# Attention and two MLP layers on one core: from interleaved attention to attention first

## The chip, the cores and the metric

One of the eight cores of a Trainium2 chip runs the whole program. The metric is device time in microseconds (us) of one execution, from the first to the last instruction plus what little lies around them. Five engines work side by side, each through its own queue in order: TensorE (PE; its weight loads are listed as PEld), VectorE (DVE), ScalarE (ACT), GpSimd (POOL) and SyncE (SP), which issues most of the DMAs. They meet at semaphores.

## The reference, cut to what matters

```
scores = scale * q @ k.T                      # 4 batches, 8 heads, 576 x 576, head size 64
scores = where(block_i >= block_j, scores, -1e9)   # blocks of 64 positions
attn   = exp(scores - max); attn = attn / (sum(attn) + 1e-9)
x      = (attn @ v) as (2304 tokens, 512)
# layer 1
h = x @ w_in;  g = h if h >= 1, 0 if h <= -1, else (h + 1)**2 / 4;  x = g @ w_out
# layer 2
h = x @ w_in2; g = h * cos(h);                                       out = g @ w_out2
```

Both layers go from 512 to 2048 and back. The four weight matrices arrive as 64-bit floats.

## The kernel before, in words

**Precision.** A 32-bit number is kept as a sum of two rounded parts, hi and lo, and a product of two numbers as hi·hi + hi·lo + lo·hi. So each MLP product is three matmuls.

**Attention.** Two heads are worked at a time: 4 batches x 4 head pairs give 16 pairs. `load` brings k, q and v of a pair; `prep` transposes k and q on TensorE and splits them: `Q[h]` holds q's hi in the head's 64 rows and its lo in the other 64, `K[h]` holds k's hi in both halves, `L[h]` holds k's lo and zeros. A pair has five units, query tiles of 128, 128, 128, 128 and 64 rows (the last holds both heads). `scores` multiplies `Q[h]` with `K[h]` (hi·hi and lo·hi in one) and with `L[h]` (hi·lo), and then adds the mask by a third, small bf16 product of `mk_l` and `mk_r` on the 64 columns that are masked. Then DVE takes the negated maximum, ACT the exponential with its sum (L373, L418), DVE the reciprocal. `p_trans` transposes the probabilities on TensorE, ACT copies them out of PSUM (L467), `pv` multiplies with v (L488). Where `late` holds, the division comes after that: a matmul with the identity spreads the reciprocals (L496) and DVE multiplies (L508); otherwise POOL scales the probabilities first (L386, L433). The result, split in hi and lo, is stored to DRAM as `x1d` (L518), one DMA per pair.

**The MLP.** Tokens are worked in blocks of 512 (and one of 256, tokens 2048 to 2303); a block has NF = 16 steps, one per 128 columns of the hidden layer. `mm1` (L596) makes one hidden tile from 12 matmuls, `act` applies the activation through ACT, DVE and POOL and splits the result into `gh` (POOL, L152) and `gl` (DVE, L155), and two steps later `mm2` (L660 in layer 1, L667 in layer 2) adds 12 matmuls into the accumulators.

**Weights.** Each of the 64 weight tiles (32 per layer) is converted from 64-bit floats by `w_convert`: ACT takes the upper words (L176) and the lower ones (L182; early ones on POOL, L178), DVE joins them in two steps (L191, L195), hi is rounded on POOL or ACT, POOL subtracts to get lo (L155). w_in of layer 1 stays in SBUF; the other three matrices go back to DRAM, and w_out is fetched again for each step through a ring of six slots (`fetch`), layer 2's w_in once.

**Order.** Each stage registers its later parts with `at(d, ...)`, due d ticks later; a tick is one piece of attention or MLP. The first 133 pieces of attention (`START`: five pairs and eight pieces) run alone with eight PSUM banks; then `zipped` runs 48 steps of layer 1 with the rest of attention between them, 1.2 and later 1.06 pieces per MLP piece, with three banks for attention and one for `h`. Then come the rest of layer 1 and layer 2. The table `jobs` says in which MLP steps a weight tile is converted: two per step in the first 14, later fewer, and none in steps 64 to 79, which are the 256-token block. From all that a scheduler makes one queue per engine, and an engine never leaves its queue's order.

## Time and profile before

| what | value |
|---|---|
| median of three runs | 1113.91 us (1112.87 to 1118.11) |
| the profiled execution | 1114.9 us, its span 1112.7 us |
| mean granted TensorE clock | 0.975 of full speed |
| busy | PE 1046.3 us, DVE 618.3, ACT 558.6, POOL 410.8 |
| moved by DMA | 200.63 MB |

How to read it: busy times are sums over the whole span, over stages that have different limits. A matmul counts as busy while it is anywhere in the pipeline, so two that overlap count their union, and a PE that is shown busy may still issue fewer columns than it could. The stages are told apart by the tables of windows further down.

### The profile page before, as it was taken

The numbers are of one execution on the slowest core, as the hardware profiler recorded it, in microseconds if no ns is written. First come the engines' busy times: TensorE is split into PE (matmuls) and PEld (weight loads), VectorE is DVE, ScalarE is ACT, GpSimd is POOL, SyncE is SP. The second block draws the span as 40 slices with busy tenths as digits, with TensorE's granted clock in tenths as the row PEclk, the third lists the DMA queues.
The fourth block names the chain that finished last, engine by engine and source line by source line (L and its number), as shares of the span: only waits on it lengthen the run. The fifth ranks groups of instructions, "written<-read, shape, count | busy, mean of one in ns | idle before, by whom it ended". The sixth has DMA issues, their size and how long they took to land.

```text
span 1112.7 us, 17002 instructions
## 1 busy us (share of the span) xinstructions
PE 1046.3 (94%) x5912; PEld 847.5 (76%) x5912; DVE 618.3 (56%) x1143; ACT 558.6 (50%) x1253; POOL 410.8 (37%) x577
## 2 busy tenths in 40 slices
PE   8888889999999979999949999899999999999998
PEld 6666667777777756777737889788888888888897
DVE  6677597676535455466507443254454454454464
ACT  6777688766445465555515433333333343343343
POOL 1234376554423444355507531132223222322322
PEclk8998999999999989999979999999999999999999
DMA  5576466557644584556786679722532442442353
GB/s 134 154 202 196 136 211 199 189 176 242 230 133 154 174 257 152 173 179 217 242 320 220 215 264 380 264 95 95 172 131 97 168 150 96 151 134 95 114 191 113
DMA packets 145572, 200.63 MB, mean 180 GB/s; under 512 B 66384, under 2 KB 107344, under 8 KB 145488
## 3 DMA queue, kind: packets, MB, share of 16 engines
q1 hardware_dynamic: 138576, 174.39, 48.8%
q0 software_dynamic: 6912, 25.17, 5.8%
q8 instruction: 47, 0.77, 0.3%
q14 instruction: 37, 0.30, 0.1%
HBM read 150.77 MB, written 48.76 MB: 179 GB/s over the span
## 4 chain that ended last, share of the span: by engine, by line
PE 72%; ACT 8%; DMA 8%; DVE 6%; issue 3%; SPq 2%; POOL 1%; POOLq 0%; ACTq 0%; DVEq 0%
PE h L596 32%; PE a L667 17%; PE a L660 12%; PE s L488 4%; DMA raw<-in_moe_w_in_dram 3%; PE s L350 3%; PE s L451 2%; DMA x1d<-xs 2%; ACT raw L182 2%; ACT raw L176 2%; ACT P L373 1%; PE s L299 1%; DVE wv L195 1%; DMA w2i<-w 1%; DVE raw L191 1%
## 5 line engine op out<-in xcount | busy, mean ns | idle before, releaser
L596 PE MATMUL h<-x,w 128*128 128x512 f32 (+1 forms) x1920 | 439.4, 377 | 28.1 <-DMA x<-x1d 13.9
L596 PEld LDWEIGHTS h<-x,w 128*128 128x128 f32 x1920 | 340.3, 192 | 95.1 <-DMA x2d<-y 14.3
L152 POOL TENSOR_SCALAR gh<-ea 128x512 fp32r<-128x512 f32 (+1 forms) x160 | 101.2, 632 | 394.1 <-DVE ea L640 177.4
L660 PE MATMUL a<-gh,w 128*128 128x512 f32 (+1 forms) x640 | 199.7, 376 | 0.0
L667 PE MATMUL a<-w,gh 128*128 128x512 f32 x576 | 174.3, 390 | 0.1
L155 DVE TENSOR_TENSOR gl<-ea,gh 128x512 fp32r<-128x512 f32 (+1 forms) x160 | 123.2, 770 | 82.5 <-POOL gh L152 81.9
L660 PEld LDWEIGHTS a<-gh,w 128*128 128x128 f32 x640 | 116.0, 189 | 18.3 <-issue 0.7
L636 ACT ACTIVATE eb<-eb 128x512 f32<-128x512 f32 (+1 forms) x80 | 47.0, 588 | 158.7 <-DVE eb L633 158.7
L667 PEld LDWEIGHTS a<-w,gh 128*128 128x128 f32 x576 | 107.1, 188 | 22.0 <-POOL gh L152 0.5
L615 ACT ACTIVATE ea<-h,half 128x512 f32<-128x512 f32 (+1 forms) x80 | 51.6, 644 | 141.4 <-PE h L596 134.6
L660 PE MATMUL a<-gl,w 128*128 128x512 f32 (+1 forms) x320 | 120.8, 377 | 0.0
L667 PE MATMUL a<-w,gl 128*128 128x512 f32 x288 | 108.4, 389 | 0.0
L640 DVE TENSOR_TENSOR ea<-h,eb 128x512 f32<-128x512 f32 (+1 forms) x80 | 50.8, 637 | 79.7 <-ACT eb L637 79.7
L629 POOL TENSOR_SCALAR ea<-ea 128x512 f32<-128x512 f32 (+1 forms) x80 | 64.1, 801 | 79.0 <-ACT ea L626 76.3
L155 POOL TENSOR_TENSOR w<-wv,w 128x512 fp32r<-128x512 f32 x64 | 87.5, 1369 | 13.1 <-ACT w L210 11.2
L191 DVE SCALAR_TENSOR_TENSOR raw<-raw 128x512 uint32<-128x512 uint32 x64 | 49.4, 772 | 74.5 <-ACT raw L182 72.2
L626 ACT ACTIVATE ea<-h,magic 128x512 f32<-128x512 f32 (+1 forms) x80 | 51.3, 642 | 78.2 <-PE h L596 64.3
L488 PE MATMUL s<-PT,rv 128*64 128x128 f32 (+2 forms) x960 | 73.8, 274 | 16.5 <-ACT P L418 6.1
L632 DVE TENSOR_TENSOR eb<-h,ea 128x512 f32<-128x512 f32 (+1 forms) x80 | 51.0, 637 | 57.3 <-POOL ea L629 57.3
L373 ACT ACTIVATE P<-s,m 128x512 f32<-128x512 f32 (+3 forms) x128 | 66.5, 524 | 31.2 <-DVE m L366 30.0
L621 DVE SCALAR_TENSOR_TENSOR ea<-ea,h 128x512 f32<-128x512 f32 (+1 forms) x80 | 50.4, 630 | 54.9 <-ACT ea L618 54.0
L488 PEld LDWEIGHTS s<-PT,rv 128*64 128x64 f32 (+1 forms) x960 | 50.5, 140 | 39.1 <-issue 10.6
(87 smaller groups left out, 1425.9 us busy)
## 6 DMA issues: line engine op xcount, KB each, us to landing
w<-w2o SPq DMA_DIRECT2D x80, 512.0 KB, 3.3
w<-w1o SPq DMA_DIRECT2D x64, 512.0 KB, 4.5
raw<-in_moe_w_in_dram SPq DMA_DIRECT2D x32, 512.0 KB, 4.7
raw<-in_moe_w_out_dram SPq DMA_DIRECT2D x32, 512.0 KB, 5.1
x1d<-xs SPq DMA_DIRECT2D x16, 576.0 KB, 4.5
x2d<-y SPq DMA_DIRECT2D x36, 256.0 KB, 6.4
x<-x2d SPq DMA_DIRECT2D x36, 256.0 KB, 5.5
w1o<-w POOLq DMA_DIRECT2D x16, 512.0 KB, 3.6
```

What stands on the lines that cost most here:

```text
L152: return nc.gpsimd.tensor_scalar(out=hi, in0=raw, scalar1=1.0, scalar2=1.0, op0=ALU.mult, op1=ALU.mult)
L155: (eng or nc.vector).tensor_tensor(out=lo, in0=raw, in1=hi.bitcast(F32), op=ALU.subtract)
L191: nc.vector.scalar_tensor_tensor(out=low.bitcast(U32), in0=top.bitcast(U32), scalar=0x80000000, in1=low.bitcast(U32), op0=ALU.bitwise_and, ...
L373: e = nc.scalar.activation(out=probs[u, h], in_=os[h], func=ACTF.Exp, bias=m[:, h:h + 1], accum_out=den[:, h:h + 1])
L488: nc.tensor.matmul(out=ps[64 * h:64 * h + 64, 0:nq], lhsT=V[0:n, j, h, :], rhs=r, start=(j == 0), stop=(j == i), skip_group_check=True,)
L596: nc.tensor.matmul(out=hps[s][:, 0:n_], lhsT=w[:, a, kk * 128:(kk + 1) * 128], rhs=x[:, b], start=(kk == 0 and n == 0), stop=(kk == NK - 1 ...
L615: P.act = nc.scalar.activation(out=g, in_=h, func=ACTF.Relu, bias=half, scale=0.5)
L626: P.act = nc.scalar.activation(out=g, in_=h, func=ACTF.Identity, bias=magic, scale=INV2PI)
L629: nc.gpsimd.tensor_scalar(out=g, in0=g, scalar1=-MAGIC, scalar2=-C1, op0=ALU.add, op1=ALU.mult)
L632: nc.vector.tensor_tensor(out=u, in0=h, in1=g, op=ALU.add)
L660: nc.tensor.matmul(out=o, lhsT=w[:, a, dm:dm + 128], rhs=b, start=(f == 0 and n == 0 and c == 0), stop=(f == NF - 1 and n == 2), skip_grou ...
L667: nc.tensor.matmul(out=A, lhsT=b[:, t], rhs=w[:, a, :], start=(f == 0 and n == 0), stop=(f == NF - 1 and n == 2))
```

## The change

Attention of all 16 pairs runs first, with all eight PSUM banks (four of its own, four that are later `h`'s). Only in the last 18 of its 368 pieces does every third piece let one MLP piece in.

- The mask moves into the second score product. `L[h]`'s zero half now holds, for the masked 64 columns of each tile, three rows' worth of mask parts, and a new tile `R[h]` holds a copy of q's hi beside ones in the fitting rows. The small third product is gone; five POOL copies per pair make `R`, and 32 small POOL operations fill the constant halves at the start.
- `late` and its matmuls and multiplications are gone: POOL scales the probabilities of all 16 pairs.
- The distance from scores to transposes grows from two units to three; more buffers: probabilities 4 and 3 instead of 3 and 2, transposed ones 2 instead of 1, `xs` 2 instead of 1. V's next load is issued one unit later (unit 3 instead of 2).
- All 32 weight tiles of layer 1 stay in SBUF: 20 in slots of their own, 12 in the space that attention leaves. Six are converted during attention instead of four. Layer 2's tiles go to DRAM and are fetched during the last block of layer 1, into layer 1's slots. `jobs` converts them in steps 16 to 46; one of two low fields goes to POOL.
- Layer 1 takes the 256-token block third, in steps 32 to 47.

```diff
@@ consts
-        nc.vector.memset(mk_l[:, 0:64], 1.0)
-        nc.vector.memset(mk_l[:, 64:128], 0.0)
-        nc.vector.memset(mk_r, 0.0)
...
+        for o in (0, 64):
+            for i in range(LAST):
+                e = ident[o:o + 64, o + nm * i:o + nm * (i + 1)]
+                t = mk_t[o:o + 64, 0:nm]
+                nc.vector.tensor_tensor(out=t, in0=e, in1=mk_p[o:o + 64], op=ALU.mult)
+                nc.vector.tensor_reduce(out=mk[o:o + 64, 0, i:i + 1], in_=t, axis=AX.X, op=ALU.add)
+                nc.vector.tensor_reduce(out=mk[o:o + 64, 1, i:i + 1], in_=e, axis=AX.X, op=ALU.add)
@@ w_convert
-            if early:
+            if early or n % 2:
...
-            if (layer, which) != (1, 0):
-                at(5, lambda: w_store(layer, f, which, t))
+            if layer == 2:
+                at(5, store)
@@ attn_pools
-        P.v, P.pt, P.xs, P.sm = sb("v", 2), sb("pt", 1), sb("xs", 1), sb("sm", 4)
-        P.raw, P.p = sb("qkr", 1), [sb("p0", 3), sb("p1", 2)]
+        P.v, P.pt, P.xs, P.sm = sb("v", 2), sb("pt", 2), sb("xs", 2), sb("sm", 5)
+        P.raw, P.p = sb("qkr", 1), [sb("p0", 4), sb("p1", 3)]
...
+                nc.vector.memset(R[h][o, :].bitcast(F32), 0.0)
+                for i in range(LAST):
+                    for t, w, c in ((L[h], 0, 128 * i + 64), (R[h], 1, 128 * i)):
+                        nc.gpsimd.tensor_scalar(
+                            out=t[o, c:c + 64], in0=ident[o, 0:64], scalar1=0.0, scalar2=mk[o, w, i:i + 1],
...
+        P.ps = [(stack.enter_context(tc.tile_pool(name="ps_s", bufs=4, space=PSUM, side="right")), "s")]
+        P.ps = (P.ps + [(M.h[0], "h")]) * 4
@@ attention
-        TL = 2
-        late = lambda u: pairs.index(u[:2]) < alone
+        TL = 3
...
+                def copied():
+                    for h in range(2):
+                        a = 64 * h
+                        for d0, d1, sh in cuts(h):
+                            d = slice(d0 + sh, d1 + sh)
+                            rounded(R[h][a:a + 64, d], Q[h][a:a + 64, d].bitcast(F32))
...
-                mm(os[h], Q[h][:, qs], L[h][:, 0:nk], start=False, stop=False)
-            for h in range(2):
-                mm(os[h][:, nk - 64:nk], mk_l, mk_r, start=False, stop=True)
+                mm(os[h], R[h][:, qs], L[h][:, 0:nk], start=False, stop=True)
...
-            if late(u):
-
-                for h in range(2):
-                    c = 0 if i < LAST else 64 * h
-                    nc.tensor.matmul(
-                        out=ps[64 * h:64 * h + 64, 128:128 + nq], lhsT=rs.pop((u, h)).to_broadcast([128, 64]),
...
@@ moe and the main order
-    blocks = [(layer, js) for layer in (1, 2) for js in halves]
+    blocks = [(1, js) for js in halves[:2] + halves[4:] + halves[2:4]] + [(2, js) for js in halves]
...
+                if (layer, js) == blocks[NBL - 1]:
+                    at(1, lambda f=f: w_fetch(f, 0))
...
-        x = NF + c * 8 // 5 if c < 20 else 3 * NF + (c - 20) * 4 // 3
+        x = NF + c * 5 // 4 if c < 25 else 2 * NF + (c - 25) * 2
...
+    for n, _ in enumerate(attention(pairs)):
+        tick()
+        if done < NA and n >= 100 + 45 * done:
+            next_weight()
+            done += 1
+        if n == total // 2:
+            x_load(steps[0], range(NK))
+        if n >= total - LEFT:
+            P.ps = own
+            P.early = False
+            if (n - total + LEFT) % 3 == 0:
+                next(mlp)
+                tick()
```

What it does to the queues shows at three places. The first is PE at the scores of a unit with 512 keys, two heads. Before, with `a` and `h` of the MLP between them (L350 the scores, L451 the transposes):

```order
L660 MATMUL a_3828<-gh,w 128x512
L451 MATMUL s<-ident,P 128x128 x4
L350 MATMUL s<-K_241,Q_239 128x512
L350 MATMUL s<-L_243,Q_239 128x512
L350 LDWEIGHTS mk_l
L350 MATMUL s<-mk_r,mk_l 128x64
L596 MATMUL h<-x,w 128x512 x10
L350 MATMUL s<-K_242,Q_240 128x512
L350 MATMUL s<-L_244,Q_240 128x512
```

The same unit in the changed kernel (L378 the scores, L508 the product with v, L318 the transposes of the next pair's q, L471 those of the probabilities):

```order
L378 MATMUL s<-K_231,Q_229 128x512
L378 MATMUL s<-L_233,R_235 128x512
L508 MATMUL s<-PT_860,rv 64x64 x2
L318 MATMUL s<-ident,rq 128x128 x2
L378 MATMUL s<-K_232,Q_230 128x512
L378 MATMUL s<-L_234,R_236 128x512
L471 MATMUL s<-ident,P 128x128 x4
L508 MATMUL s<-PT_901,rv 64x128 x2
```

The mask's load and product and all MLP matmuls have gone from between the scores; only attention's own work stands there.

The second is POOL in the 256-token block of layer 1. Before, the 16 roundings of `gh` stand there alone, behind the last conversions of block (6, 7):

```order
L152 TENSOR_SCALAR w<-wv 128x512
L155 TENSOR_TENSOR w<-wv,w 128x512
L144 DMA w2o_129<-w 128x1024
L152 TENSOR_SCALAR gh<-ea 128x512 x2
L152 TENSOR_SCALAR gh<-ea 128x256 x16
```

Now a piece of it reads so (L161 rounds, L164 subtracts, L187 takes low fields, L152 issues the store):

```order
L152 DMA w2i_99<-w 128x1024
L161 TENSOR_SCALAR w<-wv 128x512
L187 TENSOR_SCALAR raw<-raw 128x512
L161 TENSOR_SCALAR w<-wv 128x512
L161 TENSOR_SCALAR gh<-ea 128x256
L164 TENSOR_TENSOR w<-wv,w 128x512
L161 TENSOR_SCALAR gh<-ea 128x256
L164 TENSOR_TENSOR w<-wv,w 128x512
L152 DMA w2o_100<-w 128x1024
```

Between the first and the last of the 16 `gh` of this block now stand 13 subtractions, 12 roundings, 5 low fields and 11 stores of layer 2's weights.

The third is PE at the end of attention. Before, the last pair's transposes (L458, L463) and its products with v (L488) come to an end ahead of 51 matmuls of `mm1` (L596), the whole of steps 48 to 51 and a part of the next:

```order
L488 MATMUL s<-PT_6042,rv 64x128
L463 MATMUL s<-ident,P 64x128
L488 MATMUL s<-PT_6073,rv 64x64 x8
L488 MATMUL s<-PT_6095,rv 64x64 x2
L596 MATMUL h<-x,w 128x512 x51
```

Now the scores of the last pair (L378) already have the first `mm1` (L603) between them:

```order
L378 MATMUL s<-K_264,Q_262 128x384
L378 MATMUL s<-L_266,R_268 128x384
L603 MATMUL h<-x,w 128x512 x11
L508 MATMUL s<-PT_4012,rv 64x64 x8
L508 MATMUL s<-PT_4023,rv 64x64 x2
L471 MATMUL s<-ident,P 128x128 x2
L378 MATMUL s<-K_263,Q_261 128x512
L378 MATMUL s<-L_265,R_267 128x512
L603 MATMUL h<-x,w 128x512 x16
```

The scheduler lets more in than the pieces say: 96 matmuls of `mm1`, eight steps, stand ahead of attention's last product and before the first `mm2`.

## Rows read from the trace of the kernel before

**Rows 1.** The page: the span; one of its costliest groups (busy, mean ns, idle before).

```profile
span 1112.7 us, 17002 instructions
...
L660 PE MATMUL a<-gh,w 128*128 128x512 f32 (+1 forms) x640 | 199.7, 376 | 0.0
```

**Rows 2.** Windows, mm1 (L596) alone: from:to, length, PE, PEld busy (count), clock, DMA.

```profile
108.80:254.90 146.10, 52.82 (x192) 37.61 (x192) 0.96 0.58 189
254.90:388.80 133.90, 51.19 (x192) 35.81 (x193) 0.99 0.57 181
388.80:548.10 159.30, 48.76 (x192) 34.92 (x192) 0.98 0.62 204
548.10:656.60 108.50, 47.85 (x192) 36.93 (x193) 0.94 0.69 244
656.60:705.30 48.70, 25.95 (x192) 24.54 (x192) 1.00 0.94 339
705.30:795.70 90.40, 47.80 (x193) 37.05 (x194) 0.98 0.40 137
795.70:882.70 87.00, 46.41 (x193) 36.02 (x192) 1.00 0.40 134
...
1056.80:1112.70 55.90, 25.69 (x192) 25.02 (x191) 1.00 0.45 151
```

**Rows 3.** The chain of waits, one mm1 of layer 2: start, us, what.

```profile
774.06 2.72 PE h L596 x12
```

**Rows 4.** SP's queue, timeline: stores of the second and the fifth pair.

```profile
57.41 0.54 SPq L518 DMA_DIRECT2D x1d<-xs  x1
...
104.67 0.38 SPq L518 DMA_DIRECT2D x1d<-xs  x1
```

**Rows 5.** Windows of pairs one and two: PE, PEld, DVE, ACT, POOL busy, clock, DMA.

```profile
0.00:35.70 35.70, 31.81 (x252) 24.99 (x254) 24.14 (x77) 23.92 (x73) 7.79 (x21) 0.86 0.51 120
35.70:57.40 21.70, 18.56 (x162) 13.53 (x158) 15.70 (x43) 16.37 (x53) 6.24 (x10) 0.92 0.67 195
```

**Rows 6.** Windows of pairs three to five (57.40 to 104.70 us): sum and mean.

```profile
sum 47.30, PE 41.98 PEld 31.85 DVE 36.72 ACT 37.23 POOL 15.90; mean PE 13.99 PEld 10.62 DVE 12.24 ACT 12.41 POOL 5.30
```

**Rows 7.** Groups by line, 57.40 to 104.70 us, PE: busy, mean ns, idle before.

```profile
L496 PE MATMUL s<-ident,r 128*64 128x128 f32 x40 | 4.5, 273 | 0.0
L350 PE MATMUL s<-mk_r,mk_l 65*128 65x64 bf16 x24 | 3.7, 201 | 0.0
```

**Rows 8.** Groups by line, whole span, POOL: busy, mean ns, idle before.

```profile
L386 POOL TENSOR_SCALAR P<-P,r 128x128 f32<-128x128 f32 (+3 forms) x88 | 54.8, 632 | 30.6 <-DVE r L381 25.6 <-ACT ea L615 3.1 <-PE s L451 0.9
L152 POOL TENSOR_SCALAR K<-K 64x256 fp32r<-64x256 f32 (+1 forms) x64 | 30.2, 471 | 79.6 <-ACT K L307 57.4 <-PE s L451 8.8 <-PE s L488 8.3
...
L178 POOL TENSOR_SCALAR raw<-raw 128x512 uint32<-128x512 uint16 x4 | 2.6, 650 | 5.9 <-DMA raw<-in_moe_w_out_dram 4.1 <-DMA raw<-in_moe_w_in_dram 1.7
masks.py:199 POOL TENSOR_SCALAR_AFFINE_SELECT ident<-ident 128x128 f32<-128x128 f32 x1 | 0.3, 291 | 0.1
```

**Rows 9.** Timeline of POOL, 600 to 620 us: start, us, line, operation.

```profile
602.55 1.79 POOL L155 TENSOR_TENSOR w<-wv,w 128x512 fp32r<-128x512 f32 x1
...
605.90 0.60 POOL L144 DMA_DIRECT2D w2i<-w  x1
606.53 1.30 POOL L155 TENSOR_TENSOR w<-wv,w 128x512 fp32r<-128x512 f32 x1
...
614.85 0.62 POOL L152 TENSOR_SCALAR w<-wv 128x512 fp32r<-128x512 f32 x1
```

**Rows 10.** Timeline of DVE, 600 to 620 us.

```profile
603.11 1.78 DVE L155 TENSOR_TENSOR gl<-ea,gh 128x512 fp32r<-128x512 f32 x1
605.98 0.69 DVE L155 TENSOR_TENSOR gl<-ea,gh 128x512 fp32r<-128x512 f32 x1 [1.10 <-POOL gh L152]
...
613.71 0.69 DVE L195 SCALAR_TENSOR_TENSOR wv<-raw 128x512 uint32<-128x512 uint32 x1
```

**Rows 11.** Window 600 to 650 us, all engines, columns as in rows 5.

```profile
600.00:650.00 50.00, 50.00 (x222) 41.38 (x221) 26.14 (x35) 18.94 (x32) 30.77 (x34) 1.00 0.70 241
```

More of the change, by code (lines that the diff above doesn't have):

```diff
@@ L202, in joined, with store @@
                 (w_in, w_out)[which][layer, f] = t
-            else:
+            def store():
+                w_store(layer, f, which, t)
                 stage.append((pool, tag))
@@ L283, in load @@
             raws[b, p, which] = t
-            if which == 2 and 0 < n < alone:
-                load_weights(loaded[0] + 1, len(wq) // 2)
+            if which == 2 and n:
+                load_weights(loaded[0] + 1, 2 * NWA)
         def qk_of(b, p):
@@ L505, in out_ @@
                 x = X[:, 1, 128 * i:128 * i + nq]
[L506 to L510 removed]
+                nc.scalar.activation(out=x, in_=ps[:, 0:nq], func=ACTF.Copy)
             at(1, out_)
@@ L548, in attention @@
                 yield
-            which = {3: 0, 0: 1, 2: 2}.get(x % NI)
-            if which is not None and x > 0:
-                at(2, lambda n=x // NI + (2 if which == 0 else 1), which=which: load(n, which))
+            for which in {3: (0, 2), 0: (1,)}.get(x % NI, ()):
+                if x > 0 and (which != 2 or x > NI):
+                    at(2, lambda n=x // NI + (2 if which == 0 else 1), which=which: load(n, which))
     xs = {}
@@ L703, in attn_moe_moe_kernel @@
     lag = lambda s: 2 if s[0] == 1 or len(s[1]) == 2 else 3
-    def fetch(x):
-        if NF <= x < nsteps:
-            layer, js, f = steps[x]
-            w_out[layer, f] = w_fetch(layer, f, 1, ws, f"o{x % RING}")
     def moe(lo, hi):
@@ L738, in moe @@
             for y in ready:
-                at(1, lambda y=y: fetch(y + RING))
-                if y < NF:
-                    used[0] = y + 1
-                    load_weights(converted[0] + 4, 2 * NF)
-    def zipped(a, b, rates):
-        credit = 0.0
-        for t, _ in enumerate(a):
-            credit += rates[min(t // (6 * NF - 8), len(rates) - 1)]
-            while credit >= 1.0 and next(b, None) is not None:
-                credit -= 1.0
-                tick()
-            tick()
-        for _ in b:
-            tick()
-    EXTRA = 6
-    RING = 6
+                if steps[y][:2] == blocks[NBL - 1]:
+                    at(1, lambda f=steps[y][2]: w_fetch(f, 1))
     wq = [(layer, f, which) for layer in (1, 2) for f in range(NF) for which in range(2)]
@@ L762, in load_weights @@
         while loaded[0] < min(upto, limit):
-            layer, f, which = wq[loaded[0]]
-            if layer == 1 and which == 1 and f >= RING and used[0] < f - RING + 1:
-                break
-            if layer == 2 and not stage:
+            if wq[loaded[0]][0] == 2 and not stage:
                 break
@@ L803, in attn_moe_moe_kernel @@
     attn_pools(attn_st)
-    a1 = attention([(b, p) for b in range(B) for p in range(NP)], NP + NX)
-    with ExitStack() as st:
-        own = P.ps
-        P.ps = own + [(st.enter_context(tc.tile_pool(name="ps_s1", bufs=4, space=PSUM)), "s")] * 4 + [(M.h[0], "h")]
-        done = 0
-        for n in range(START):
-            next(a1)
-            tick()
-            if n >= 40 and done < NA and (n - 40) * NA // 70 >= done:
-                next_weight()
-                done += 1
-            if n == START - 20:
-                x_load(steps[0], range(NK))
-        flush()
-        P.ps = own
@@ L819, in attn_moe_moe_kernel @@
-    M.a = ctx.enter_context(tc.tile_pool(name="ps_a", bufs=1, space=PSUM))
-    P.early = False
-    load_weights(converted[0] + 4, 2 * NF)
-    pieces = moe(0, NF * (B - 1))
-    zipped(pieces, a1, RATES)
+    pairs = [(b, p) for b in range(B) for p in range(NP)]
+    total = len(pairs) * (2 * 3 + (NI - 3) * 4 + 5 + 4)
+    own = [p for p in P.ps if p[1] == "s"]
+    mlp = moe(0, nsteps + 3)
+    done = 0
+    for n, _ in enumerate(attention(pairs)):
[11 more added lines that the diff above has]
+                tick()
@@ L836, in attn_moe_moe_kernel @@
+    M.y = ctx.enter_context(tc.tile_pool(name="y", bufs=1))
+    with ExitStack() as st:
+        wc = st.enter_context(tc.tile_pool(name="wc", bufs=1))
+        stage += [(wc, f"c{c}") for c in range(6)]
+        load_weights(converted[0] + AHEAD, len(wq))
+        while turn[1] <= 3 * NF:
+            next(mlp)
+            tick()
     M.u = ctx.enter_context(tc.tile_pool(name="u", bufs=2))
-    for f in range(EXTRA):
-        w_in[2, f] = w_fetch(2, f, 0, wx, f"x{f}")
-    for _ in moe(n, nsteps + 3):
+    for _ in mlp:
```

109 lines of the change are left out of this document (44 added, 65 removed).

## The prediction

> **What bounds the kernel now.** I began with the windows that run from the first `mm1` of one MLP block to that of the next. A 512-token block of layer 2 takes 87.0 us, the same with and without neighbours, and its 16 steps are 24 matmuls each, 12 of which take 2.72 us: 16 x 2 x 2.72 = 87.0 [rows 2, 3]. So there TensorE's issue alone sets the time. The three blocks that have attention between them take 146.1, 133.9 and 159.3 us, the fourth, at whose start attention ends, 108.5 [rows 2]. That is 547.8 us for four blocks worth 348.2 and for 11 of the 16 pairs (the fifth pair's store leaves at 104.67, just ahead of these windows [rows 4]). The extra 199.6 us are 18.1 per pair.
>
> Then I looked at the pairs that run alone. Between the stores of pairs two and five lie 47.3 us, 15.8 per pair [rows 4], with the clock at full speed and PE shown busy for 14.0 us of each, ACT for 12.4, DVE for 12.2, POOL for 5.3 [rows 6]. No engine fills its pair; the four take turns. So a pair alone costs 15.8 us and a pair between MLP pieces 18.1. Mixing them, as the kernel does, hides nothing.
>
> **The change as a sum.** The new time is a start, 16 pairs, both layers, less what overlaps at the seam, plus what weight conversion adds.
>
> *Start.* The second store leaves at 57.4 us [rows 4], 25.8 later than two pairs at 15.8 would need. To that come 32 mask fills on POOL, priced by the nearest row at 0.29 us [rows 8], of which 15 stand ahead of the first copies into `R`: 15 x 0.29 = 4.4 us, some of it while the first loads still fly, so I take 4 (0 to 9.3, all 32). The third unit of distance between scores and transposes delays the last store by one unit, a fifth of a pair: 3 us. Together 33.
>
> *A pair.* On PE the mask products go (8 per pair, 24 rows of 201 ns in three pairs: 1.2 us shown busy) and so do the spreading products (40 of 273 ns, 10.9 us summed but 4.5 us of time taken: 1.5 per pair) [rows 7]; PE shows at most 11.3 us then. ACT keeps its 12.4: `late` had one ACT copy per unit and the new order has one too. POOL gains: nine scalings of probabilities at 0.63 (the widest a little more) are 5.7 us, five copies into `R` at 0.47, the price of the like-shaped `K` rounding, 2.4 [rows 8]. That makes 5.3 + 8.1 = 13.4 us per pair, more than ACT's. This work lies beside ACT's and PE's, and the third unit of distance and the extra buffers are its cover. If the cover fails, all of it stands in the path: 15.8 + 8.1 = 23.9. The other end is the fullest engine that was there before, ACT: 12.4. I take 14.8: 1.0 less than the row of pairs alone, since PE loses 2.7 us and `xs`, transposed probabilities and probabilities get a further buffer each, but clear of POOL's 13.4, since no engine of that row came nearer its pair than 14.0 of 15.8. 16 x 14.8 = 236.8.
>
> *Both layers alone.* Four blocks at 87.0, the 256-token block at 48.7, layer 2's first block at 90.4 with its seam, three at 87.0 and the last with the end at 55.9 [rows 2]: 348.0 + 48.7 + 90.4 + 261.0 + 55.9 = 804.0. That layer 1's w_out is no longer stored and fetched is worth nothing here: no `mm2` of layer 1 ever waited, L660's idle time is 0.0 [rows 1].
>
> *Seam.* The order puts 96 `mm1` matmuls, 8 x 2.72 = 21.8 us, ahead of attention's last product. From there to the last store attention alone would need about 17 us (six units, the last ones light); its own PE work in them, two thirds of a pair, is 8 us. With the MLP's 21.8 beside it PE has 30 us to do, all useful, so the layers end 17 - 8 = 9 us before store + 804; I take 8 (0 to 17).
>
> *Conversion.* Layer 1's last 26 tiles are now converted two per step in steps of 5.44 us. Alone, POOL needs per step two subtractions at 1.30, a low field at 0.65 and `gh` at 0.62 [rows 8, 9]: 3.9 us, so nothing is added. But POOL and DVE do not run quite apart. A subtraction takes 1.30 us at 606.53 and 1.79 at 602.55, while DVE's `gl`, 0.69 at 605.98, takes 1.78 at 603.11, started in the middle of that subtraction and ended just behind it [rows 9, 10]. If the two always took turns, a step would need another five DVE operations of 0.69: 7.3 us, 1.9 over the step, 24 us in 13 steps. In the 256-token block the order has 13 subtractions, 12 roundings at 0.62, 11 store issues at 0.60, 5 low fields and 16 `gh` of at most 0.62: 44.1 us of POOL, inside the block's 48.7; with 32 joins and 16 `gl` taking turns, 33 us more, 28 over. So conversion costs 0 to 52. With 12 tiles in 16 steps, and these same collisions, PE still issued 222 matmuls in 50 us, its full rate [rows 11], so I stay near the low end: 15.
>
> The Trainium skill's page "SBUF — State Buffer", section "Who interferes with whom", says that VectorE and GpSimd share one pair of ports, and that a VectorE operation with two inputs in SBUF and a GpSimd operation that reads SBUF exclude each other for their whole length. The collision above agrees with it, and by that rule without any slack conversion would cost the full 52.
>
> Sum: 33 + 236.8 + 804 - 8 + 15 = 1080.8 us of span. The profiled execution had 2.2 us around its span and lay 1.0 above the median of the runs, so the forecast is 1082 us, 2.9% below 1113.9. In short, span = 829 + 16 P + C, with P the pair and C the conversion. By the same form the old span is reached at P = 16.8 with C = 15, or at C = 47 with P = 14.8.
>
> **Rivals.**
> - *A deep pipeline.* The buffers let a pair run at the fullest engine's pace, P = 13.5, and conversion hides in the slack of two steps between `mm1` and `mm2`, C = 5: 829 + 216 + 5 + 1 = 1051. For it: rows 11 lose nothing. Against it: eight PSUM banks served the lone pairs before too, and each engine was idle for a ninth to two thirds of a pair [rows 6].
> - *Port-bound conversion.* C is all of 52: 829 + 236.8 + 52 + 1 = 1119. For it: the two lengthened rows and a table that packs 12 tiles and more into a block of half length. Against it: three steps of weights are ready when the layer begins.
> - *Slower: the clock falls while attention runs alone.* PE would be shown busy for 11.3 of 14.8 us. In the first two pairs it was granted 0.86 and 0.92 [rows 5], after the long first wait; from 57 us on, 1.00. At half the clock a pair needs up to 22.6 us of PE. If it falls in half of the time, P = 18: 829 + 288 + 15 + 1 = 1133. It decides from P = 16.8 on. Against it stand 47 us at full clock with the same transposes and products.
> - *Slower: POOL sets the pace.* It holds 13.4 us in a queue where k's rounding, `R` and the probabilities wait behind each other, and each stretch where DVE blocks it is lost; P = 17.5 gives 829 + 280 + 15 + 1 = 1125. Against it: three units of slack.
>
> **How the numbers follow.** The forecast has 0.52 (its own range 1062 to 1104: P from 14 to 16, C from 5 to 25), the deep pipeline 0.20, port-bound conversion 0.10, the clock 0.09, POOL 0.09. No change means within 0.5%, 1108.3 to 1119.5, about what a measurement of this kernel can tell. Faster: 0.52 + 0.20 and a third of the port case, 0.75. Within: half of the port case and the mild part of the slow ones, 0.08. Slower: 0.17. The range from 1050 to 1122 leaves out part of the deep pipeline and the worse half of the slow cases.
>
> **What the profile would show.** The stores of pairs three to fifteen tell P: 14.8 apart on the mean, 13.5 or 17.5 by the rivals; POOL near 13 us per pair and ACT near 12.4; the clock at 1.00 after the first 50 us. The first `mm1` stands near 253 us, and the last store, with the head start ahead of it, near 283. The first block of layer 1 takes up to 10 us more than 87 after the head start of eight steps is added back, the 256-token block up to 10 more than 48.7, all other blocks 87.0, and layer 2's last block ends as before. I am wrong if a pair takes 16.8 or more, if the blocks of layer 1 together lose more than 47 us, or if blocks without conversions are no longer 87.0.

## The result: 1086.7 us, 2.4% faster, and the profile after

The changed kernel takes 1086.7 us (median of 4 runs, 1084.8 to 1089.3) against 1113.4 for the kernel before (4 runs); the ratio is 0.9757, 95% interval [0.9716, 0.9797]. The forecast was 1082. The profiled execution took 1088.05 us with a span of 1086.3.

The page first: the span, busy time and share of TensorE, and two of the costliest groups (busy, mean ns, idle before and who ended most of it).

```profile
span 1086.3 us, 16454 instructions
...
PE 1035.3 (95%) x5684; PEld 849.2 (78%) x5684; DVE 634.0 (58%) x1147; ACT 534.5 (49%) x1220; POOL 506.7 (47%) x751
...
L603 PE MATMUL h<-x,w 128*128 128x512 f32 (+1 forms) x1920 | 426.8, 369 | 4.6 <-POOL w L164 2.9
...
L471 PE MATMUL s<-ident,P 128*128 128x128 f32 x320 | 61.9, 316 | 26.0 <-POOL P L409 17.9
```

L603 is `mm1`. TensorE is idle for 1086.3 - 1035.3 = 51.0 us. About half of that stands in front of L471, the transposes of the probabilities: 26.0 us, 17.9 of them until GpSimd had scaled P (L409). The windows from one block's first `mm1` to the next one's, as in [rows 2] (length, PE, PEld, clock, DMA):

```profile
261.00:370.90 109.90, 49.74 (x192) 36.67 (x193) 0.95 0.30 105
370.90:458.00 87.10, 46.48 (x193) 36.06 (x193) 1.00 0.54 187
458.00:506.40 48.40, 25.79 (x192) 24.25 (x191) 1.00 0.84 286
506.40:595.60 89.20, 47.24 (x193) 35.80 (x194) 1.00 0.36 124
595.60:682.60 87.00, 46.73 (x192) 36.00 (x192) 1.00 0.64 214
...
1030.80:1086.30 55.50, 25.34 (x192) 24.79 (x191) 0.99 0.08 29
```

Every block is now at its lone length but the first, in which the end of attention and 26 conversions stand (89.2 us is the block behind the 256-token one, 90.4 in [rows 2]). From the first `mm1` to the end it is 825.3 us. Attention comes out less even. The stores of `x1d` in SP's queue, as in [rows 4]; the second leaves where it did before:

```profile
57.37 0.37 SPq L525 DMA_DIRECT2D x1d<-xs  x1
...
71.28 0.37 SPq L525 DMA_DIRECT2D x1d<-xs  x1
...
84.13 0.57 SPq L525 DMA_DIRECT2D x1d<-xs  x1
...
101.41 0.37 SPq L525 DMA_DIRECT2D x1d<-xs  x1
...
251.11 23.59 SPq L525 DMA_DIRECT2D x1d<-xs  x2
309.02 0.38 SPq L525 DMA_DIRECT2D x1d<-xs  x1
```

From the second store to the fourteenth it is 193.7 us, 16.1 per pair, but single gaps run from 12.9 to 19.2. The windows of all twelve pairs, of the fourth and of the fifth say why (PE, PEld, DVE, ACT, POOL busy, clock, DMA):

```profile
57.40:251.10 193.70, 171.51 (x1432) 132.05 (x1428) 140.35 (x359) 157.28 (x513) 130.41 (x243) 0.92 0.52 146
71.30:84.10 12.80, 12.80 (x119) 9.95 (x117) 10.53 (x30) 12.44 (x42) 8.85 (x17) 1.00 0.64 172
84.10:101.40 17.30, 13.82 (x107) 11.07 (x107) 10.59 (x28) 11.05 (x38) 11.57 (x22) 0.80 0.68 198
...
85.00:88.90 3.90, 1.51 (x17) 1.17 (x15) 3.42 (x9) 1.23 (x5) 3.46 (x7) 1.00 0.98 297
88.90:95.70 6.80, 5.70 (x24) 4.75 (x24) 2.46 (x7) 3.93 (x14) 3.83 (x8) 0.50 0.64 191
95.70:101.40 5.70, 5.70 (x57) 4.42 (x58) 3.84 (x11) 5.01 (x19) 3.46 (x7) 1.00 0.49 118
```

In the fourth pair TensorE is busy for all of 12.8 us at full clock. In the fifth it first stands still, and then runs at a granted clock of 0.50, its lower level, from 88.9 to 95.7. GpSimd's timeline at that place (start, us, what):

```profile
83.41 1.76 POOL L161 TENSOR_SCALAR R<-Q 64x256 fp32r<-64x256 f32 x2
85.36 0.62 POOL L161 TENSOR_SCALAR w<-wv 128x512 fp32r<-128x512 f32 x1 [0.19 <-POOL R L161]
85.95 1.14 POOL L161 TENSOR_SCALAR R<-Q 64x320 fp32r<-64x320 f32 x3
87.17 1.26 POOL L164 TENSOR_TENSOR w<-wv,w 128x512 fp32r<-128x512 f32 x1
88.52 0.64 POOL L187 TENSOR_SCALAR raw<-raw 128x512 uint32<-128x512 uint16 x1
89.25 1.36 POOL L409 TENSOR_SCALAR P<-P,r 128x512 f32<-128x512 f32 x2
```

and TensorE's:

```profile
85.48 1.03 PE L508 MATMUL s<-PT,rv 128*64 128x128 f32 x12
90.00 1.12 PE L471 MATMUL s<-ident,P 128*128 128x128 f32 x4 [3.48 <-POOL P L409]
```

GpSimd has no gap over 0.2 us. Ahead of the scaling stand two weight operations of one conversion, one of another (0.62 + 1.26 + 0.64 = 2.5 us) and the copies into `R`. TensorE waits 3.5 us for the scaling. The same happens behind all six conversions that stand in attention: waits of 3.48, 3.83, 4.00, 3.59, 2.74 and 4.00 us (21.6 in all), each with a stretch at half clock in it or just behind it. For two of them the profile names an operation of VectorE (L406, L435) that ended within 0.1 us of the scaling.

GpSimd's queue is not all of it. The scaling also needs the reciprocal (L407), and VectorE, which joined the fields of the weight tile shortly before (0.89 us at 84.02), has no gap either:

```profile
87.59 0.86 DVE L435 TENSOR_TENSOR tm<-tm 128x1 f32<-128x1 f32 x1
88.37 0.15 DVE L407 RECIPROCAL r<-den 128x2 f32<-128x2 f32 x1
```

The reciprocal ends at 88.52, 0.7 us before the scaling starts; at the six places it is 0.7, 1.3, 2.5, 1.6, 0.7 and 1.2 us, 8.1 in all. So GpSimd's queue by itself can account for at most 8.1 of the 21.6 us of waits; for the rest the reciprocal was not there yet. The conversion holds VectorE up by more than its joins: L435 takes 0.15 to 0.18 us in the other 15 pairs, and here it ends 0.02 us behind GpSimd's subtraction (87.17 + 1.26).

### The profile page after: what moved, and what is told of

It reads as the page before. It is cut to its first block, busy times and chain, and to the rows that moved or that the text cites. A ratio compares the mean times of both kernels' runs of the same rounds, so it can differ in the third digit from the quotient of the medians.

```text
span 1086.3 us, 16454 instructions
## 1 busy us (share of the span) xinstructions
PE 1035.3 (95%) x5684; PEld 849.2 (78%) x5684; DVE 634.0 (58%) x1147; ACT 534.5 (49%) x1220; POOL 506.7 (47%) x751
## 4 chain that ended last, share of the span: by engine, by line
PE 77%; DVE 9%; POOL 5%; issue 4%; DMA 2%; ACT 2%; SPq 0%; POOLq 0%; ACTq 0%; DVEq 0%
PE h L603 32%; PE a L674 18%; PE a L667 14%; PE s L508 5%; PE s L471 4%; PE s L378 3%; PE s L318 1%; DVE raw L200 1%; DVE Q L355 1%; DVE m L392 1%; DVE wv L204 1%; POOL w L164 1%; DVE gl L164 1%; POOL P L409 1%; POOL gh L161 1%
## 5 line engine op out<-in xcount | busy, mean ns | idle before, releaser
L603 PE MATMUL h<-x,w 128*128 128x512 f32 (+1 forms) x1920 | 426.8, 369 | 4.6 <-POOL w L164 2.9
L603 PEld LDWEIGHTS h<-x,w 128*128 128x128 f32 x1920 | 337.8, 189 | 66.5 <-POOL w L164 3.1
L161 POOL TENSOR_SCALAR gh<-ea 128x512 fp32r<-128x512 f32 (+1 forms) x160 | 105.0, 656 | 381.9 <-DVE ea L647 206.3
L667 PE MATMUL a<-gh,w 128*128 128x512 f32 (+1 forms) x640 | 194.5, 371 | 3.0 <-POOL gh L161 3.0
L164 DVE TENSOR_TENSOR gl<-ea,gh 128x512 fp32r<-128x512 f32 (+1 forms) x160 | 128.3, 803 | 91.8 <-POOL gh L161 91.3
L674 PEld LDWEIGHTS a<-w,gh 128*128 128x128 f32 x576 | 107.0, 188 | 22.0 <-POOL gh L161 0.5
L164 POOL TENSOR_TENSOR w<-wv,w 128x512 fp32r<-128x512 f32 x64 | 93.3, 1460 | 18.0 <-ACT w L221 16.1
L636 POOL TENSOR_SCALAR ea<-ea 128x512 f32<-128x512 f32 (+1 forms) x80 | 71.4, 892 | 62.2 <-ACT ea L633 58.2
L409 POOL TENSOR_SCALAR P<-P,r 128x128 f32<-128x128 f32 (+3 forms) x128 | 70.0, 559 | 44.6 <-DVE r L407 15.6
L471 PE MATMUL s<-ident,P 128*128 128x128 f32 x320 | 61.9, 316 | 26.0 <-POOL P L409 17.9
L508 PE MATMUL s<-PT,rv 128*64 128x128 f32 (+2 forms) x960 | 79.7, 272 | 0.4 <-ACT PT L487 0.2
L200 DVE SCALAR_TENSOR_TENSOR raw<-raw 128x512 uint32<-128x512 uint32 x64 | 54.5, 857 | 42.9 <-ACT raw L191 25.2
L392 DVE TENSOR_REDUCE m<-s 128x2 f32<-128x256 f32 (+2 forms) x96 | 57.2, 599 | 29.2 <-PE s L378 27.9
```

Of the source, the lines that this page charges most:

```text
L161: return nc.gpsimd.tensor_scalar(out=hi, in0=raw, scalar1=1.0, scalar2=1.0, op0=ALU.mult, op1=ALU.mult)
L164: (eng or nc.vector).tensor_tensor(out=lo, in0=raw, in1=hi.bitcast(F32), op=ALU.subtract)
L200: nc.vector.scalar_tensor_tensor(out=low.bitcast(U32), in0=top.bitcast(U32), scalar=0x80000000, in1=low.bitcast(U32), op0=ALU.bitwise_and, ...
L392: nc.vector.tensor_reduce(out=m[:, hs[0]:hs[-1] + 1], in_=o, axis=AX.X, op=ALU.max, negate=True)
L409: nc.gpsimd.tensor_scalar(out=probs[u, h], in0=probs[u, h], scalar1=r[:, h:h + 1], scalar2=1.0, op0=ALU.mult, op1=ALU.mult)
L471: nc.tensor.transpose(ps[:, w * x + j * 128:w * x + (j + 1) * 128], pr[:, j * 128:(j + 1) * 128], ident)
```

## The experiments

Times are medians; the kernel before stood at 1115.8, 1116.5, 1114.9 and 1116.8 on the four chips that these runs came from, and at 1113.4 beside the changed kernel. Differences between experiments are good to about 3 us.

**1. The conversions early.** Theory A: a conversion in attention holds up GpSimd's queue, TensorE waits for P, and its clock falls behind the wait. Rival B: the clock falls in lone attention by itself. Rival C, taken up in experiment 3: it is GpSimd's whole load, not the conversions. All six conversions go to the first two pairs:

```diff
-        if done < NA and n >= 100 + 45 * done:
+        if n == 2:
+            load_weights(NA, 2 * NWA)
+        if done < NA and n >= 8 + 6 * done:
```

> The changed kernel with the six weight conversions of attention moved into its first two pairs (from piece 8 on, one every 6 pieces, instead of one every 45 from piece 100). Theory A: each conversion puts some 2.5 us of POOL work ahead of the probabilities that TensorE waits for, TensorE stands still for 2.7 to 4.0 us, and its clock is at 1.2 GHz for the next 3.4 to 6.8 us. Then no such wait and no low clock should be seen between 60 and 250 us, pairs three to fourteen should be 13 to 15 us apart (now 16.1 on the mean), and the span should fall by 15 to 24 us less up to 8 us in the first two pairs: 1063 to 1077 us. Rival B: the clock falls in lone attention by itself, because TensorE issues too little there: at least four low stretches remain between 60 and 250 us and the span stays at 1080 to 1090.

1063.9 us (1062.3 to 1064.8), ratio 0.9537 [0.9523, 0.9551]. The window of its pairs 3 to 14, columns as above:

```profile
69.90:233.20 163.30, 159.31 (x1426) 122.16 (x1424) 131.12 (x344) 151.91 (x503) 111.81 (x229) 1.00 0.54 147
```

A pair takes 163.3 / 12 = 13.6 us instead of 16.1, TensorE is busy for 98% of it, and in these pairs the clock never falls, so B is out. The edit moves the whole conversion, its parts on ScalarE and VectorE too, so it shows that the conversions are the cause and not through which queue. The price is at the start: the first store leaves at 53.0 instead of 43.1 and the second at 69.9 instead of 57.4, 12.5 us later, where A allowed for 8.

**2. Less of a conversion on GpSimd.** The low fields and the rounding of attention's conversions go to ScalarE; GpSimd keeps the subtraction.

```diff
-            if early or n % 2:
+            if n % 2 and not early:
...
-                if early or layer == 2:
+                if layer == 2:
```

> The changed kernel with the conversions of attention at their old places, but their low fields and their rounding on ACT, so that POOL has only the subtraction (1.3 us instead of 2.5 us per tile). Theory A: the six waits of TensorE shrink to 1 to 2.5 us and the clock falls at three places or fewer; span 1070 to 1081. Rival B: still six low stretches, span 1083 to 1090. If ACT, not POOL, is what the probabilities wait for, the waits grow instead and the span is over 1090.

1074.1 us (1070.2 to 1074.2), ratio 0.9621 [0.9602, 0.9641]: A's time, but not its signs. From 60 to 240 us TensorE waits 14.6 us for P instead of 20.3, with a longest wait of 3.4 us where A had 2.5; five low stretches remain between 60 and 250 us where A had at most three, and four of them are half as long as most were. With half of GpSimd's part gone, over two thirds of the waiting stays, as the late reciprocals let expect.

**3. The mask as a product of its own again.** No `R`, no copies, no fills, a third product.

```diff
...
-                mm(os[h], R[h][:, qs], L[h][:, 0:nk], start=False, stop=True)
+                mm(os[h], Q[h][:, qs], L[h][:, 0:nk], start=False, stop=False)
+            for h in range(2):
+                mm(os[h][:, nk - 64:nk], mk_l, mk_r, start=False, stop=True)
```

> The changed kernel with the mask as a third small product again and without the copies into R: 2.4 us less of POOL and 8 more small products on TensorE per pair, no mask fills at the start. Theory A: between conversions no queue of POOL sets the pair, so a pair changes by less than 0.4 us, the six low stretches stay, and only the start gets 3 to 6 us shorter: span 1077 to 1087. Rival C: POOL's load sets the pace of a pair; with 2.4 us less a pair loses 0.8 us or more, span 1063 to 1075. If the product removed was worth its 1.2 us of busy time per pair, the span grows to 1095 or more.

1072.8 us (1069.1 to 1075.7), ratio 0.9627 [0.9599, 0.9655]: this part of the change costs 14 us where it stands. The first store leaves at 34.4 us instead of 43.1, so the fills cost about 9. A pair takes 15.6 us instead of 16.1, between what A and C forecast. Without the copies no wait for P between 50 and 240 us is over 1.8 us, and three low stretches are left there of the six that A expected. So C has a share: the conversions stand in line with the copies.

**4. The order alone.** The kernel before with all 368 pieces of attention ahead of layer 1 and nothing else changed.

```diff
-    START = 25 * (NP + NX) + 8
+    START = 16 * (2 * 3 + (NI - 3) * 4 + 5 + 4)
```

> The kernel before with one thing changed: all 368 pieces of attention run before the first step of the MLP (its mask, buffers, weight ring and block order stay; the division comes after the product for the first five pairs, as before). Theory: the order carries the gain. By the sum of the forecast, start 26, 16 pairs at 15.8 to 16.5, both layers 804, conversion 10 to 25, no head start at the seam: 1093 to 1129, most likely 1100, so it gives half of the gain or more. Rival: the gain comes from buffers, mask and resident weights, and the order alone changes nothing or loses: 1110 or more.

A miss: 1170.2 us (1164.6 to 1173.4), ratio 1.0486 [1.0454, 1.0519], in the rival's range but not by the rival's cause. Attention is not the main loss; the last store leaves at 295.1 us. Layer 1's four 512-token blocks take 422.9 us instead of 348. The first row of TensorE's waits (total, times, longest) has the cause, the read of the only PSUM bank that `mm1` has:

```profile
PE h L596 <- DVE ea L621: 40.0, 34, 4.6
```

**5. The order and the banks.** In addition the attention's banks are given back before layer 1, and `mm1` gets four.

```diff
...
+    next(a1, None)
+    flush()
+    attn_st.close()
+    M.h = M.h + [ctx.enter_context(tc.tile_pool(name="ps_h2", bufs=3, space=PSUM))] * 3
...
-    M.h += [ctx.enter_context(tc.tile_pool(name="ps_h1", bufs=3, space=PSUM))] * 3
```

> The kernel before with all attention ahead of layer 1 (run e4_order_only, 1170.2) and in addition four PSUM banks for the first product of layer 1 instead of one, got from the attention's banks. Theory H (of the 55 us that the order alone lost, 40 are waits of the first product's bank for VectorE's read, which layer 1 hid behind pieces of attention before): blocks of layer 1 under 100 us each after the first, 1120 to 1135. Rival I (the loss is from the weights: half of layer 1's output weights go out to DRAM and come back in a ring of six, and twice two conversions stand in a step): the waits turn into waits for weights, 1150 to 1172.

1107.0 us (10 runs, 1102.8 to 1109.7), ratio 0.9919 [0.9893, 0.9944], better than H's range; I's waits for weights did not come. The banks bring 63 us, more than the 40 of visible waits. The windows of the same four blocks (`mm1` alone, as in [rows 2]):

```profile
289.30:377.80 88.50, 47.21 (x193) 35.77 (x194) 1.00 0.47 161
377.80:470.10 92.30, 46.43 (x194) 36.03 (x193) 1.00 0.81 281
470.10:560.20 90.10, 46.95 (x193) 36.04 (x193) 1.00 0.79 272
560.20:647.20 87.00, 46.74 (x192) 36.01 (x192) 1.00 0.75 256
```

**6. The third unit, taken away.** The kernel of experiment 1 with `TL = 2` in place of 3, buffers left.

> The kernel of run e1_conv_early (1063.9) with two units between scores and transposes instead of three, all buffers left. Theory M (the third unit is what lets TensorE run through: with it TensorE was busy 175.1 of 180 us from 60 to 240; with two, the normalised P comes too late by about one unit): waits of L471 for POOL P of 0.5 to 1.5 us at two to four places a pair, pairs of 15 to 16.5 us instead of 13.6, 1085 to 1110. Rival N (the banks and buffers alone did it, and the third unit only adds to start and end): pairs of 13.4 to 14 us, 1060 to 1066.

1141.6 us (1140.8 to 1143.9), ratio 1.0235 [1.0194, 1.0276]: 78 us slower than experiment 1 and outside M's range on the far side. Pairs 3 to 14:

```profile
73.50:303.80 230.30, 184.68 (x1428) 143.57 (x1428) 123.59 (x349) 154.84 (x505) 108.92 (x228) 0.85 0.38 105
```

and TensorE's waits between 60 and 240 us:

```profile
PE s L471 <- POOL P L409: 17.7, 9, 2.0
PE s L508 <- ACT PT L487: 16.7, 16, 1.5
```

A pair takes 19.2 us. TensorE now waits in every pair for P and for PT, and the clock falls once per pair: 0.85 on the mean.

**7. The third unit, added alone.** The kernel of experiment 5 with `TL = 3` and one more set of the small vectors; P, PT and the output keep their old number of tiles.

> The kernel of run f4_order_and_banks (the kernel before with all attention first and four banks for layer 1's first product, 1107.0) with three units between scores and transposes instead of two, and one more set of the small vectors; the tiles of P, PT and the output stay 3, 2, 1 and 1, since the old places of the weights leave no room for more. Theory M (the third unit is the largest part of the change's gain in attention, as run g3_two_units has it, 78 us without it): the pairs after the fifth 14 to 15.5 us instead of 17.4, 1072 to 1090. Rival O (three tiles of P hold a unit back, so that the third unit is worth nothing without the fourth tile, which only the new place of the weights gives room for): the exponential waits for the transposes, pairs 17 to 19 us, 1100 to 1125.

1086.5 us (1083.9 to 1089.5), ratio 0.9725 [0.9682, 0.9768], in M's range. The pairs from the fifth store to the fourteenth:

```profile
104.80:237.90 133.10, 125.36 (x1138) 93.92 (x1138) 94.88 (x264) 114.05 (x375) 66.35 (x128) 1.00 0.39 105
```

are 14.8 us each, against 17.2 in experiment 5, and the third unit brings 20.5 us here, not the 78 of experiment 6. The order, the banks and the third unit give as much as the whole change; its other parts together come to nothing that shows.

**8. The gap filled.** 60 small products of zeros ahead of the six transposes that waited. They write the tile that the transposes overwrite.

```diff
+    FILLED = ((1, 0, 3), (1, 2, 2), (2, 0, 2), (2, 2, 2), (3, 0, 2), (3, 2, 2))
...
+            if hs[0] == 0 and u in FILLED:
+                for _ in range(60):
+                    nc.tensor.matmul(out=ps[:, 0:128], lhsT=zz, rhs=zz, start=True, stop=True, skip_group_check=True)
```

> The changed kernel with 60 small matmuls of zeros put in front of those six transposes of P that waited 2.7 to 4.0 us on GpSimd behind a weight conversion; their results are overwritten by the transposes. They take nothing from the other engines and fill TensorE's idle time with some 3.3 us of work. Theory A (the wait costs twice, once as idle time and once as the half clock of the 3.4 to 6.8 us that follow it): no stretch at granted clock 0.5 at these six places, waits as long as before, 1076 to 1083, since of six low stretches about 1.5 us each come back. Rival E (the low clock costs nothing, since a pair runs at the pace of ScalarE and GpSimd there): the clock stays at 1.00 and the time at 1085 to 1089. Rival F (the clock falls for another reason than the idle time): the low stretches stay, 1086 to 1092.

1077.1 us (1074.8 to 1082.1), ratio 0.9664 [0.9614, 0.9713], as A has it; E and F are out. Pairs 3 to 14:

```profile
62.30:247.70 185.40, 180.06 (x1734) 139.94 (x1730) 140.46 (x358) 155.00 (x510) 129.48 (x242) 1.00 0.55 150
```

The clock stays at 1.00, and twelve pairs take 185.4 us instead of 193.7. Five of the six low stretches and 19.2 us of the six waits lie in the changed kernel's window of these pairs; the sixth wait ends behind it. The window is 30.4 us longer than that of experiment 1: 18.2 us of it are idle time (193.70 - 171.51 against 163.30 - 159.31) and 12.2 are busy time that TensorE is shown longer for the same work, part of it at half the clock. Filling the gaps gave back 8.3. So the waits are worth 18 to 22 us and the clock 8 to 12.

**9. The scaling late in all pairs.** It is moved behind the product with V again, as the kernel before had it in its first five pairs, but in all 16 (`late(u)` true everywhere).

> The changed kernel with the normalisation moved behind the product with V in all 16 pairs, as the kernel before had it in its first five: GpSimd loses the ten normalising operations of a pair (about 5.7 us), TensorE gets ten products of 128 rows, VectorE five to six products. Theory A (GpSimd's normalisation stands between the exponential and TensorE's transposes, so each conversion that GpSimd does in attention pushes it): the six waits of 2.7 to 4.0 us go, no low clock behind them, pairs 13.6 to 15.0 us, 1064 to 1078. Rival G (TensorE and VectorE set the pace, GpSimd only at the six conversions): pairs 15.5 to 16.5 us, 1080 to 1095.

1065.8 us (1065.7 to 1067.3), ratio 0.9559 [0.9517, 0.9602]. Pairs 3 to 14:

```profile
56.20:237.00 180.80, 180.03 (x1702) 138.20 (x1699) 145.32 (x427) 157.47 (x515) 70.64 (x139) 1.00 0.58 161
```

15.1 us per pair: 1.5 more than in experiment 1, which is what the spreading products were priced at [rows 7], and no wait over 0.2 us between 60 and 240 us, although the conversions stand where they stood. So a conversion costs only where the division stands between the exponential and the transposes, and taking `late` out cost 21 us where it stands. The edit takes both the scaling on GpSimd (nine operations a pair: 144 in 16 pairs) and the reciprocal on VectorE off that path; which of the two queues counts for how much was not tried.

**10. Early and mask apart.** Experiments 1 and 3 together.

> The changed kernel with two edits of earlier runs together: the six conversions of attention in its first two pairs (run e1_conv_early, 1063.9) and the mask as a third product again, without R and its copies (run e3_mask_apart, 1072.8). Theory A (VectorE, ScalarE and TensorE set a pair at about 13.5 us once GpSimd is never late, and the fills of the mask at the start cost their 9 us besides): stores of pairs 2 to 13 13.0 to 13.8 us apart, first store near 44, 1050 to 1058. Rival B (early conversion and mask apart relieve the same queue, GpSimd's, so that with one the other brings only the start): 1054 to 1062. Rival D (the third product comes back on TensorE's path once GpSimd no longer hides it, 10 short matmuls a pair, about 1 us): pairs of 14.5 us, 1064 to 1072.

1058.4 us (1056.8 to 1059.0), ratio 0.9488 [0.9445, 0.9530], in B's range and just outside A's: the best version here with experiment 11, 28 us under the changed kernel. Pairs take 13.9 us, 0.3 more than in experiment 1, and the first store leaves at 41.9 instead of 53.0. The two gains, 23 and 14, do not add up, which fits B: both relieve one queue.

**11. Four conversions early.** As experiment 10 with `NA = 4`.

> The kernel of run f1_early_and_apart (1058.4) with four conversions in the first two pairs instead of six, so that the first block converts 28 pieces of weight in 14 steps instead of 26 in 13. Theory A (a conversion ahead of the first block costs more than one in it: six early ones set the first store from 34.4 to 41.9 us, 1.2 us each, while the first block loses some 12 us over 26): first store near 39.5, the first block half a us to 1 us longer, 1054 to 1058. Rival J (the first block is limited by how early its weights come, so that each conversion fewer ahead of it makes TensorE wait at its first steps): waits of L580 for POOL w of over 4 us in all, first block 3 to 6 us longer, 1059 to 1064.

1058.4 us (1055.0 to 1064.2), ratio 0.9491 [0.9443, 0.9540]: no difference. The first store leaves 3.5 us earlier and the first block is as long (106.9 us from its first product against 107.0), so J is out, but the pairs give the start back (14.4 us each).

**12. No seam.** As experiment 10, with layer 1 begun behind the last piece of attention (`LEFT = 0`).

> The kernel of run f1_early_and_apart (1058.4) in which layer 1 begins only when the last piece of attention has been issued (no steps of layer 1 between the last 18 pieces of attention). Theory K (the interleaving hides the last pair's chains, worth the 8 us that the prediction gave to it, and the 12 us that the first block is over are its conversions'): the first block 97 to 100 us from its first product, 1062 to 1068. Rival L (the first block is over because TensorE's work of attention stands in it and its conversions cost next to nothing, as in run f4_order_and_banks, where a first block with 28 conversions and no attention in it took 88.5 us): first block 88 to 91 us, and the time at 1056 to 1062, the seam being worth 0 to 4 us.

1063.0 us (1061.2 to 1063.2), ratio 0.9522 [0.9477, 0.9566]: the seam is worth 4.6 us by the medians, though the intervals of the two ratios overlap. The first and the 256-token block (`mm1` alone):

```profile
247.20:345.50 98.30, 46.70 (x192) 36.02 (x193) 0.98 0.33 110
432.60:481.00 48.40, 25.83 (x193) 24.29 (x192) 1.00 0.86 290
```

and TensorE's waits in the first:

```profile
PE a L644 <- DVE gl L158: 7.1, 10, 1.7
PE a L644 <- POOL gh L155: 1.5, 2, 0.8
```

With next to no attention in it the first block is 11.3 us over 87.0, most of it waits for `gl`. That is what K forecast, and the lengthened `gl` (last section) points to the conversions. L's ground stays: in experiment 5 a first block with 26 of its 28 conversions in it took 88.5 us, and the loss came in the second and third block instead (5.3 + 3.1). Why it falls there is open.

## Why the prediction was right, step by step

The sign, the size and the outline (start, pairs, layers alone) were right. The nearness of the total is in part luck: twelve pairs at 16.1 instead of 14.8 us are 16 us late, and a start that was 5 us shorter than forecast gave a third of that back. Put into the prediction's own form, 829 + 16 x 16.1 + 15 would be 1102. The sum by its two halves:

| part | forecast | measured |
|---|---|---|
| first `mm1` | 253 | 261.0 |
| from there to the end | 1080.8 - 253 = 827.8 | 825.3 |
| last store | 283 | 309.0 |

*What bounds.* By its rows a mixed pair did cost more than a lone one. But that mixing hides nothing was wrong in one respect: it hid that `mm1` had a single bank (next paragraph). The 18.1 per mixed pair is somewhat too low, since the first of the sixth pair's pieces stand ahead of those windows; it enters no term.

*The layers, 804.* Right: behind the first block 87.1, 48.4, 89.2, five at 87.0 or 87.1 and 55.5 at the end answer to [rows 2]. What the sum took for granted is the banks. The order alone would have made the kernel 54 us slower (experiment 4); the change brings the four banks with it, and no rival of the prediction thought of their absence.

*Conversion, 15.* About right: 11.3 in the first block of experiment 12's kernel, and nothing behind it there or in the changed kernel. The 256-token block, for which the upper bound had 28, lost nothing with 12 subtractions in it. The collision of [rows 9, 10] is there all the same: `gl` took 1.59 us on the mean in experiment 12's first block against 0.69 in a block of layer 2. Where fewer conversions stand (13 in the second block, 12 in the 256-token one), the blocks stay at 87.1 and 48.4 us; that the two steps between `mm1` and `mm2` hold it is an explanation, not tried. The rule of the Trainium skill's page "SBUF — State Buffer", section "Who interferes with whom", that such operations exclude each other, agrees with the lengthened `gl`; the 52 us that it would have cost without slack did not come. The rival is out. The range that the prediction gives itself, 1062 to 1104, is narrower than the corners of its own terms, 1059 (P = 14, C = 5) and 1111 (P = 16, C = 25).

*Seam, 8.* It was 4.6 where it was tried. The last store stands 26 us behind the forecast, 48 behind the first `mm1` instead of 30: the `mm1` of nine steps, the `mm2` of two and 11 conversions lie between them. What is lost there is part of the 22.9 us by which the changed kernel's first block exceeds 87.0, and was not measured apart.

*Start, 33.* The second store, due at 33 + 2 x 14.8 = 62.6, left at 57.4. The fills and copies cost 9 us at the first store and 7.5 at the second instead of 4 (experiment 3), and the rest of the start was shorter by more.

*A pair, 14.8.* This is the mis-sized term: 16.1, just above the prediction's own range of 14 to 16. The step that failed is "clear of POOL's 13.4, since no engine of that row came nearer its pair than 14.0 of 15.8", together with what the sum left out. TensorE was to shrink to 11.3 us and GpSimd to be the fullest with 13.4. In experiment 1 TensorE is shown busy for 159.3 / 12 = 13.3 us of a pair and GpSimd for 111.8 / 12 = 9.3. GpSimd's 5.3 us of [rows 6] were not attention's alone; in that window of the kernel before stand (busy, mean ns, idle before)

```profile
L155 POOL TENSOR_TENSOR w<-wv,w 128x512 fp32r<-128x512 f32 x3 | 3.8, 1275 | 0.2
...
L386 POOL TENSOR_SCALAR P<-P,r 128x128 f32<-128x128 f32 (+1 forms) x4 | 1.7, 424 | 0.2
```

which are conversions and the next pair's scalings. With the third unit TensorE fills 98% of a pair (experiment 1), and an undisturbed pair is 13.6 us, nearly the 13.5 of the deep pipeline; so the value taken was 1.2 too high. But the six conversions in attention were priced at nothing, and each stops TensorE for 2.7 to 4.0 us and lowers its clock: 30.4 us in the window of twelve pairs, 2.5 per pair. Two errors of opposite sign left 1.3.

*The signs.* GpSimd took 130.4 / 12 = 10.9 us per pair with its conversions, not 13, ScalarE 13.1 instead of 12.4, and the clock did not stay at 1.00 behind the first 50 us. The first block kept its sign: 61.9 us from the last store to its end, and with the 131 MLP products ahead of that store (29.7 us at 2.72 for 12) 91.6, inside the 10 us allowed over 87.

*The rivals.* "A deep pipeline" was near on the pair, once the conversions were out of the way: 13.6 us and 1063.9 in experiment 1, 1058.4 in experiment 10, against 1051 forecast; but TensorE was the fullest engine, not GpSimd. "POOL sets the pace" was wrong on how and right on where: GpSimd is busy for two thirds of the time, and what stands ahead of the scaling in its queue, and of the reciprocal in VectorE's, delays TensorE. "The clock falls while attention runs alone" had its mechanism wrong: between conversions lone attention ran at 1.00 (experiments 1 and 9), and the clock fell at the waits. A time near its price came where the third unit is missing, 1141.6 us against 1133 forecast, with 19.2 us per pair at a clock of 0.85; waits of 3.7 us per pair are in it too.

*What the change holds.* Three of its choices cost time where they stand: the places of the six conversions (23 us, experiment 1), the mask in the second product (14 us, experiment 3) and the scaling in front (21 us, experiment 9). They act through the same queues, so their sum means little. The late fetch, the resident weights, the further tiles of P, PT and the output and the new order of blocks were not tried by themselves. Experiment 7 has none of these, keeps the mask apart, divides late in five pairs and converts its four early tiles within them, and is as fast. So together they gain about what the three choices cost together, and how much that is stays open.

## What to carry to other kernels

When work is moved to an engine with idle time, look at its queue and not at its share: what counts is what stands there ahead of the one operation that the full engine waits for, and in the queue of the engine that feeds that operation. Here a wait of TensorE was paid twice, as idle time and as the low clock with it. What one more unit in flight is worth depends on the rest: 78 us in the kernel of experiment 1, 20.5 in that of experiment 5; the banks were worth 63. And an overlap that is taken away may have hidden a resource that is too small: price the new order with the old number of banks before crediting the order.

## What the runs showed of the hardware that was not expected

- Towards the end of waits of 2.7 to 4.0 us in the middle of dense work, or just behind them, the granted clock fell to 0.50 (1.2 GHz) and came back by itself; the stretches were 3.4 to 6.8 us long. In experiment 6 it fell in the same way at two waits of 1.5 and 2.0 us in a pair. Products of zeros in the wait kept it at 1.00 (experiment 8), at no cost that shows.
- In the first block VectorE suffers from the conversions more than GpSimd. Groups by line in the first block of experiment 12 (busy, mean ns, idle before):

```profile
L158 POOL TENSOR_TENSOR w<-wv,w 128x512 fp32r<-128x512 f32 x26 | 39.9, 1535 | 12.7 <-ACT w L215 12.3
...
L158 DVE TENSOR_TENSOR gl<-ea,gh 128x512 fp32r<-128x512 f32 x15 | 23.8, 1587 | 6.9 <-POOL gh L155 6.9
```

and a block of layer 2 in the changed kernel, from 603 to 690 us:

```profile
L164 DVE TENSOR_TENSOR gl<-ea,gh 128x512 fp32r<-128x512 f32 x16 | 11.1, 692 | 13.9 <-POOL gh L161 13.9
```

  `gl` more than doubles, while the subtraction goes from 1.30 [rows 9] to 1.54.
